# Where a feed-forward's squares lie, and when its result sums are taken, in a fused attention kernel

## The chip, the core and the metric

The kernel runs on one core of one Trainium2 chip. The metric is the device time of one execution in microseconds (us); the kernel before takes 1431.97 us (median of three runs, 1430.68 to 1434.18). A core has TensorE (PE: matmuls into PSUM), VectorE (DVE), ScalarE (ACT), GpSimd (POOL) and SyncE (SP, which here issues the DMAs). Each engine works through its own instructions in the program's order, and semaphores hold an instruction back until its inputs and its output's buffer are ready.

## The reference

Two blocks follow each other. The first is attention with a threshold: of each row of scores only those within tau of the row's maximum are kept. The second normalizes the features, multiplies by two weight matrices with a relu between, and adds the result to its input.

```python
# q, k, v: (8, 8, 576, 64)                                  (cut)
scores = scale * np.matmul(q, k.transpose(0, 1, 3, 2))
thresh = np.max(scores, axis=-1, keepdims=True) - tau
scores = np.where(scores >= thresh, scores, -1000000000.0)
attn = softmax(scores)                       # written out in the original
x = (attn @ v) as (8, 576, 512)
mu = np.mean(x, axis=-1, keepdims=True)
var = np.mean((x - mu) ** 2, axis=-1, keepdims=True)
xn = (x - mu) / np.sqrt(var + 1e-06) * g_ln
ch = np.maximum(xn @ w_ch1, 0.0) @ w_ch2     # (512, 2048), (2048, 512)
return x + ch
```

## The kernel before

The attention of a batch is cut into nine **slots**, 72 in all. A slot does scores (TensorE), the rows' negated maximum `neg` (VectorE), exponentials `e` (ScalarE), threshold and sum (VectorE), the scaling of `e` (GpSimd), and a transpose: `et` on VectorE, written to DRAM as `scr` and read back as `em` in the next slot, where TensorE multiplies it with `v`. Slots are named by batch and step, (2,7) for instance.

The feed-forward of half a batch (a **group** of 288 tokens, 16 groups) is fed to TensorE in small portions between the slots' own matmuls. Group 2b runs its first part from slot (b,6) on, group 2b+1 from slot (b+1,2) on. Scores have PSUM banks of their own; all the rest share a ring of two banks, the tag `ff`.

The first part makes 16 tiles of `hidden`, takes the squares, and at some tile the variance. The reciprocal root follows on VectorE in three steps:

```python
    def first_part(g):
        ...
            nc.scalar.activation(hidden[:, d], p1, func=AF.Relu)
            ...
            if d == (1 if plain else 5):
                sq = ffn.tile([128, NK, TOK], F32, tag="sq", bufs=1, name="sq")
                nc.scalar.activation(sq, xc, func=AF.Square)
                for c in range(1, NK):
                    nc.gpsimd.tensor_tensor(out=sq[:, 0], in0=sq[:, 0], in1=sq[:, c], op=ALU.add)
            if d >= (8 if plain else 11) and rb is None and (part or d == ND - 1):
                var = ps_ff.tile([128, TOK], F32, tag="ff", name="var")
                product(var, lhsT=avg_sb, rhs=sq[:, 0], start=True, stop=True)
                rb = ffn.tile([128, TOK], F32, tag="rb", bufs=2, name="rb")
                nc.scalar.activation(sq[:, 1], var, func=AF.Identity, bias=eps_sb)
                aside.append(lambda: root(rb, sq[:, 1], sq[:, 2]))
                yield 1, 1
```

The second part multiplies by quarters, in seven products instead of eight. The sums of the seven results go into a tile `y`, which has the same tag `sq`, one buffer. They are put into a list, and `drip` deals them out at the end of the slots' quarters, up to 5 or 6 of those that are old enough. `finish` multiplies by the root and adds x; `store` transposes one quarter of the features into a tile `ot`; the sends of all `ot` are issued on SyncE early in the next slot, behind the load of `em`:

```python
    def store(g, m, o):
        ot = ffn.tile([128, TOK], F32, tag="o", bufs=4, name="ot")
        nc.vector.transpose(ot, o)
        stores.append(lambda: send(g, m, ot))
    ...
    # in each slot                                          (cut)
        run(n, 0)                 # em of the slot before is fetched
        run_all(stores)           # then the sends
        second_part(n, 0)
        ...                       # q and k of a later pair: load_qk
        scr = turn_blocks(s, es)  # et, and its write to scr
        drip(5)
        ...                       # v of a later pair: load_v
        second_part(n, 3)
        run_all(aside)
        drip(6)
```

Of the kernel before, what the change touches and what calls it, by code (L numbers as in the profile page):

```python
# [8 lines left out]
F32 = mybir.dt.float32  # L9
# [3 lines left out]
ALU = mybir.AluOpType  # L13
AF = mybir.ActivationFunctionType
# [4 lines left out]
def kernel(  # L19
# [31 lines left out]
    nc = tc.nc  # L51
# [5 lines left out]
    NK = DM // 128  # L57
    ND = DF // 128
    J = 4
    NB = S // 32  # L60
    TOK = S // 2
# [12 lines left out]
    ffn = ctx.enter_context(tc.tile_pool(name="ffn", bufs=2))  # L74
# [6 lines left out]
    eps_sb = consts.tile([128, 1], F32, name="eps_sb")  # L81
# [8 lines left out]
    hidden = consts.tile([128, ND, TOK], F32, name="hidden")  # L90
# [508 lines left out]

    aside, stores, drops = [], [], []  # L600

    def drip(most):


        urgent = [i for i, d in enumerate(drops) if d[0]]
        old = sum(d[1] < now for d in drops)
        n = max(min(most, old), urgent[-1] + 1 if urgent else 0)
        for _ in range(n):
            drops.pop(0)[-1]()

    def run_all(calls):
        now = calls[:]
        calls.clear()
        for fn in now:
            fn()

    def add_to_x(g, m, p2, rb):
        o = ffn.tile([128, TOK], F32, tag="o", bufs=4, name="o")
        nc.vector.tensor_mul(o, p2, rb)
        nc.gpsimd.tensor_tensor(out=o, in0=o, in1=groups[g][:, m], op=ALU.add)  # L620
        aside.append(lambda: store(g, m, o))

    def store(g, m, o):
        ot = ffn.tile([128, TOK], F32, tag="o", bufs=4, name="ot")
        nc.vector.transpose(ot, o)  # L625
        stores.append(lambda: send(g, m, ot))

    def send(g, m, ot):
# [57 lines left out]
    def first_part(g):  # L686


        xc = centred.pop(g)
        rb = sq = None  # L690
        plain = g == 0
        sums_of = differences() if g == 1 else iter(())
        for d in range(ND):
            while conversion.ended < 4 * (d // 4 + 1):
                yield 0, 0
            p1 = ps_ff.tile([128, TOK], F32, tag="ff", name="p1")
            for c in range(NK):
                product(
                    p1, lhsT=w1_sb[c][:, d * 128 : (d + 1) * 128], rhs=xc[:, c],
                    start=(c == 0), stop=(c == NK - 1),  # L700
                )
                if c < NK - 1:
                    yield 1, 1
            nc.scalar.activation(hidden[:, d], p1, func=AF.Relu)  # L704
            next(sums_of, None)
            yield 2, 1
            if d == (1 if plain else 5):
                sq = ffn.tile([128, NK, TOK], F32, tag="sq", bufs=1, name="sq")
                nc.scalar.activation(sq, xc, func=AF.Square)
                for c in range(1, NK):  # L710
                    nc.gpsimd.tensor_tensor(out=sq[:, 0], in0=sq[:, 0], in1=sq[:, c], op=ALU.add)
            if d >= (8 if plain else 11) and rb is None and (part or d == ND - 1):

                var = ps_ff.tile([128, TOK], F32, tag="ff", name="var")
                product(var, lhsT=avg_sb, rhs=sq[:, 0], start=True, stop=True)
                rb = ffn.tile([128, TOK], F32, tag="rb", bufs=2, name="rb")
                nc.scalar.activation(sq[:, 1], var, func=AF.Identity, bias=eps_sb)
                aside.append(lambda: root(rb, sq[:, 1], sq[:, 2]))
                yield 1, 1
        for _ in sums_of:  # L720
            pass
        return rb
# [16 lines left out]
    def second_quarters(g, rb):  # L739

        s2, s3, s4 = more
        b11, b12 = hidden[:, :HD, early], hidden[:, :HD, late]
        b21, b22 = hidden[:, HD:, early], hidden[:, HD:, late]
        y = ffn.tile([128, NK, TOK], F32, tag="sq", bufs=1, name="y")
        part_of = lambda t, i, j: t[:, HM * i : HM * i + HM, (early, late)[j]]
        y11, y12, y21, y22 = (part_of(y, i, j) for i in range(2) for j in range(2))
        done = set()  # L750

        def later(*calls, urgent=None):
            for what, fn, *args in calls:

                def go(what=what, fn=fn, args=args):
                    fn(*args)
                    done.add(what)

                drops.append((urgent, now, go))

        def need(*what):
            while not done.issuperset(what):
                drops.pop(0)[-1]()

        def by_fours(eng, out, in0, in1, op):
            for d in range(0, HD, 4):
                at = (slice(None), slice(d, d + 4))
                eng.tensor_tensor(out=out[at], in0=in0[at], in1=in1[at], op=op)  # L768

        def segment(weights, rhs, out=None):  # L770
            bank = ps_ff.tile([128, HM, HT], F32, tag="ff", name="seg")
            for d in range(HD):
                for m in range(HM):
                    at, end = (d, m), (HD - 1, HM - 1)
                    product(
                        bank[:, m], lhsT=weights[:, m, d], rhs=rhs[:, d],
                        start=at == (0, 0), stop=at == end,
                    )
                    if at != end:
                        yield 2, 0.5  # L780
            if out is None:
                out = ffn.tile([128, HM, HT], F32, tag="part", bufs=4, name="part")
            nc.scalar.copy(out, bank)  # L783
            return out

        def add(eng, out, a, b):
            eng.tensor_tensor(out=out, in0=a, in1=b, op=ALU.add)  # L787

        def finish(eng, i, j=None):

            cols = slice(None) if j is None else (early, late)[j]
            at = (slice(None), slice(HM * i, HM * i + HM), cols)
            z, x = y[at], groups[g][at]
            r = rb[:, cols].unsqueeze(1).to_broadcast(list(z.shape))
            eng.tensor_tensor(out=z, in0=z, in1=r, op=ALU.mult)  # L795
            add(eng, z, z, x)

        dve, pool = nc.vector, nc.gpsimd
        later(("t3", by_fours, pool, b12, b22, b12, ALU.subtract), urgent=pool)
        banks_taken[0] = True  # L800
        yield from segment(w2[0, 0], b11, y11)
        need("t3")
        later(("t2", by_fours, dve, b11, b11, b12, ALU.add), urgent=dve)
        yield 2, 0.5
        p2 = yield from segment(w2[0, 1], b21)
        need("t2")
        later(("t4", by_fours, pool, b21, b21, b11, ALU.subtract), urgent=pool)
        yield 2, 0.5
        p7 = yield from segment(s3, b12)
        yield 2, 0.5  # L810
        yield from segment(s2, b11, y21)
        need("t4")
        later(("t1", by_fours, dve, b11, b22, b11, ALU.subtract), urgent=dve)
        later(
            ("u2", add, pool, y21, y21, y11), ("11", add, pool, y11, y11, p2),
            ("done11", finish, pool, 0, 0),
        )
        yield 2, 0.5
        p4 = yield from segment(w2[1, 1], b21)
        yield 2, 0.5  # L820
        need("t1", "u2", "11")
        p5 = yield from segment(w2[1, 0], b11)
        later(
            ("u4", add, dve, y12, y21, p5), ("u3", add, dve, y21, y21, p7),
            ("22", add, dve, y22, y21, p5), ("21", add, dve, y21, y21, p4),
            ("hi", finish, pool, 1),
        )
        yield 2, 0.5
        last = segment(s4, b22)
        for _ in range(6):  # L830
            yield next(last)
        banks_taken[0] = False
        while waiting_mean:
            mean_of(waiting_mean.pop(0))
        p3 = yield from last
        later(("12", add, dve, y12, y12, p3), ("done12", finish, dve, 0, 1))
        later(*((f"o{m}", store, g, m, y[:, m]) for m in range(NK)))
        yield 2, 0.5

    def ffn_steps(g):  # L840
# [78 lines left out]
    for n in range(NS):  # L919
# [30 lines left out]
        blocks_go = by_blocks(b * HP)  # L950
        diags = weights(es, thr, blocks_go)
        run_all(aside)
        drip(0)
        if n < SLOTS:
            run_all(stores)
        tick(3)
# [21 lines left out]
        if s in (HP, 2 * HP):  # L978
            group_ready(2 * b + (s > HP))
        run_all(aside)  # L980
        drip(5)
        conversion.fetch(2)
        tick(5)
        run(n, 3)
# [4 lines left out]
        second_part(n, 3)  # L989
        tick(6)  # L990
        run_all(aside)
        drip(6)
    while later_calls or queue or aside or stores or drops:
        n += 1
        for i in range(QUARTERS):
            run(n, i)
            second_part(n, i)
            run_all(aside)
            drip(99)
            run_all(stores)  # L1000


# [28 lines left out]
```

## Time and profile before

| | before |
|---|---|
| median time, us | 1431.97 |
| profiled execution, span, us | 1430.3 |
| TensorE busy | 1346.8 us, 94% |
| VectorE, GpSimd, ScalarE busy | 972.4, 591.5, 461.2 us |
| mean granted TensorE clock | 0.986 |
| TensorE's matmuls: first part (p), quarters (seg, three groups) | 528.8 us; 245.8, 123.1 and 63.9 us |
| a slot's neg, in two halves | 1.35 us each |
| an exponential of one of four blocks | 0.74 us |
| relu of one tile; squares of a group | 0.41; 1.16 us |
| a result sum y<-y,part on VectorE; on GpSimd | 0.46; 1.03 us |
| a multiplication by the root of half the features, on GpSimd | 1.48 us |
| a transpose ot | 0.45 us |

A row of a timeline reads: start, length, engine, line, operation, output and inputs, shapes, how many records, and in brackets how long the engine stood idle before it and what ended that. One product of 288 columns is four records of p, 0.516 us (528.8 us by 1024 products); one of 144 columns is four records of seg, 0.256 us. SPq is SyncE's queue of DMA issues: its times are those of issuing, and the landing comes later.

### The profile page before, as it was taken

Reading aid. Unit: us, or ns where it says so; the run is one execution under the profiler, and the core shown is the slowest. Engines: PE = TensorE matmul, PEld = TensorE weight load, DVE = VectorE, ACT = ScalarE, POOL = GpSimd, SP = SyncE. Lnnn points to the kernel's source line nnn. Section 1 sums busy time; section 2 is a strip of 40 time slices with the busy share of each in tenths; the row PEclk is TensorE's granted clock in tenths of the full one; section 3 lists DMA queues with packets and bytes.
Section 4 is the critical chain, followed back from the end, with each engine's and each line's share of the span. In section 5 each row is a group of like instructions: output and inputs, shape, how many; then the busy total and the mean of one; then the engine's idle time right before and its main releaser. Section 6 shows DMA issues by size and latency. Waiting matters only on the chain.

```text
span 1430.3 us, 35964 instructions
## 1 busy us (share of the span) xinstructions
PE 1346.8 (94%) x15048; PEld 995.7 (70%) x15048; DVE 972.4 (68%) x1668; ACT 461.2 (32%) x923; POOL 591.5 (41%) x779
## 2 busy tenths in 40 slices
PE   4889999999999999999999999999999999999996
PEld 3665666857768586867768586776858577685976
DVE  5997958667766677676765777666766677666231
ACT  3886523222222323232232323223232223223120
POOL 2344435534434353443534444433635344343222
PEclk9999999999999999999999999999999999999998
DMA  9622457557864778557864677647775577545211
GB/s 227 174 70 83 91 135 185 143 128 164 180 155 129 157 171 178 153 131 176 185 157 134 155 158 174 162 133 162 173 169 149 139 168 182 142 134 134 68 18 18
DMA packets 466866, 205.53 MB, mean 144 GB/s; under 512 B 275024, under 2 KB 428368, under 8 KB 466704
## 3 DMA queue, kind: packets, MB, share of 16 engines
q1 hardware_dynamic: 461936, 202.64, 59.4%
q8 instruction: 118, 1.93, 0.6%
q10 hardware_dynamic: 4736, 0.59, 0.4%
q14 instruction: 44, 0.36, 0.1%
q0 software_dynamic: 32, 0.00, 0.0%
HBM read 119.41 MB, written 83.76 MB: 142 GB/s over the span
## 4 chain that ended last, share of the span: by engine, by line
PE 73%; DVE 11%; DMA 6%; ACT 4%; SPq 3%; issue 2%; POOL 1%; DVEq 0%; ACTq 0%; POOLq 0%
PE p L101 30%; PE seg L101 24%; PE sc L542 8%; PE sc L385 8%; DMA em<-scr 3%; DVE e L417 2%; DVE y L787 2%; ACT e L410 2%; DVE neg L399 2%; DMA scr<-et 1%; PE tp L101 1%; DVE xc L593 1%; SPq L504 1%; DMA v_in<-in_v_dram 1%; DVE y L795 1%
## 5 line engine op out<-in xcount | busy, mean ns | idle before, releaser
L101 PE MATMUL p<-xc,w 128*64 128x288 f32 x4096 | 528.8, 413 | 28.8 <-ACT hidden L704 26.5
L101 PEld LDWEIGHTS p<-xc,w 128*64 128x64 f32 x4096 | 297.1, 139 | 241.3 <-ACT hidden L704 40.1
L399 DVE TENSOR_REDUCE neg<-sc 128x2 f32<-128x1152 f32 x144 | 188.5, 1350 | 259.6 <-PE sc L385 259.6
L410 ACT ACTIVATE e<-sc,neg 128x576 f32<-128x576 f32 x288 | 196.5, 743 | 267.6 <-DVE neg L399 267.6
L433 POOL TENSOR_SCALAR e<-e,den 128x576 f32<-128x576 f32 x252 | 197.0, 793 | 164.4 <-DVE den L422 164.4
L101 PE MATMUL seg<-hidden,w 128*64 128x144 f32 x3840 | 245.8, 287 | 0.0
L101 PEld LDWEIGHTS seg<-hidden,w 128*64 128x64 f32 x3840 | 235.1, 137 | 8.8 <-issue 6.3
L417 DVE SCALAR_TENSOR_TENSOR e<-sc,thr,e 128x576 f32<-128x576 f32 x288 | 222.0, 810 | 12.2 <-ACT e L410 11.5
L704 ACT ACTIVATE hidden<-p 128x288 f32<-128x288 f32 x256 | 104.6, 412 | 249.1 <-PE p L101 248.7
L385 PE MATMUL sc<-kT,qT 64*128 64x192 f32 (+3 forms) x1024 | 148.9, 424 | 20.0 <-DVE qT L345 10.4
L498 DVE STREAM_TRANSPOSE et<-e 128x1152 f32<-128x1152 f32 x112 | 153.2, 1374 | 12.7 <-POOL e L433 10.9
L403 POOL TENSOR_SCALAR thr<-neg,low_sb 128x2 f32<-128x2 f32 x144 | 42.2, 293 | 280.7 <-DVE neg L399 272.7
L385 PEld LDWEIGHTS sc<-kT,qT 64*128 64x128 f32 x1024 | 94.1, 190 | 70.1 <-issue 16.9
L542 PE MATMUL sc<-em,v_in 128*64 128x256 f32 (+1 forms) x1408 | 131.1, 329 | 6.0 <-DMA em<-scr 6.0
L101 PE MATMUL seg<-hidden,stage 128*64 128x144 f32 x1920 | 123.1, 286 | 0.1
L101 PEld LDWEIGHTS seg<-hidden,stage 128*64 128x64 f32 x1920 | 117.9, 137 | 3.8 <-issue 2.3
L542 PEld LDWEIGHTS sc<-em,v_in 128*64 128x64 f32 x1408 | 86.8, 137 | 40.1 <-DVE ot L625 2.3
L768 POOL TENSOR_TENSOR hidden<-hidden 128x576 f32<-128x576 f32 x60 | 85.8, 1449 | 24.7 <-ACT hidden L704 15.1
L568 POOL TENSOR_TENSOR sum<-sum,x 128x256 f32<-128x256 f32 (+1 forms) x64 | 33.0, 515 | 110.8 <-ACT x L559 108.3
L783 ACT COPY part<-seg 128x288 f32<-128x288 f32 x75 | 30.0, 400 | 145.7 <-PE seg L101 141.4
L768 DVE TENSOR_TENSOR hidden<-hidden 128x576 f32<-128x576 f32 x60 | 48.0, 835 | 33.5 <-PE seg L101 33.5
L559 ACT COPY x<-sc 128x256 f32<-128x256 f32 x60 | 22.3, 372 | 145.2 <-PE sc L542 131.0
(153 smaller groups left out, 1201.6 us busy)
## 6 DMA issues: line engine op xcount, KB each, us to landing
scr<-et SPq DMA_DIRECT2D x252, 288.0 KB, 4.9
em<-scr SPq DMA_DIRECT2D x63, 1024.0 KB, 5.9
out_dram<-ot SPq DMA_DIRECT2D x256, 36.0 KB, 1.9
q_in<-in_q_dram SPq DMA_DIRECT2D x124, 72.0 KB, 5.1
k_in<-in_k_dram SPq DMA_DIRECT2D x120, 72.0 KB, 3.1
v_in<-in_v_dram SPq DMA_DIRECT2D x64, 128.0 KB, 4.5
rest<-scr SPq DMA_DIRECT2D x63, 128.0 KB, 6.0
w<-in_moe_w_ch_dram SPq DMA_DIRECT2D x10, 512.0 KB, 5.8
```

What stands on the lines that cost most here:

```text
L101: nc.tensor.matmul(out[r], lhsT=lhsT[:, r], rhs=rhs, **flags)
L385: nc.tensor.matmul(sc[h][64 * i : 64 * i + 64 if s == HP else 128, at : at + n], lhsT=ql[r] if s == HP else qT[r, half, j * 128 : (j + 1) ...
L399: nc.vector.tensor_reduce(out=neg[:, i], in_=pairs[h], axis=AXL.X, op=ALU.max, negate=True,)
L403: nc.gpsimd.tensor_scalar(out=thr[:, i], in0=neg[:, i], scalar1=-1.0, scalar2=low_sb, op0=ALU.mult, op1=ALU.add,)
L410: nc.scalar.activation(es[:, i], blocks[i], func=AF.Exp, bias=neg[:, i : i + 1])
L417: nc.vector.scalar_tensor_tensor(out=es[:, i], in0=blocks[i], scalar=thr[:, i : i + 1], in1=es[:, i], op0=ALU.is_ge, op1=ALU.mult, accum_o ...
L433: nc.gpsimd.tensor_scalar(out=es[:, i], in0=es[:, i], scalar1=den[:, i : i + 1], scalar2=1.0, op0=ALU.mult, op1=ALU.mult,)
L498: nc.vector.transpose(et[:, :, 64 * h : 64 * h + 64].rearrange("p n (j c) -> p j n c", j=2), es[:, 2 * h : 2 * h + 2].rearrange("p j (n c) ...
L542: nc.tensor.matmul(dst[64 * h : 64 * h + 64], lhsT=vt[:, c, h, :] if c < J else vr[:, h, :], rhs=pick(em[:, c] if c < J else er, hp, h), s ...
L568: nc.gpsimd.tensor_tensor(out=sums[g][:, cols], in0=x[:, 0, cols] if c == 1 else sums[g][:, cols], in1=x[:, c, cols], op=ALU.add,)
L704: nc.scalar.activation(hidden[:, d], p1, func=AF.Relu)
L768: eng.tensor_tensor(out=out[at], in0=in0[at], in1=in1[at], op=op)
```

## The change

The squares are no longer kept in a tile of their own: they go into the last four tiles of `hidden`, which the first part fills only later. They are taken after tile 1, and the variance is asked for from tile 7 on. What ScalarE makes of the variance, and the root's second scratch tile, are new tiles `std` of the tag `o`. So `y` has its buffer to itself for longer, and the sums can be dealt out over two slots. Each entry of the list now has an engine and a cost, and a slot's end has room for 4 units on VectorE and 6 on GpSimd, then 2 and 0. The last multiplication (`done12`) moves from VectorE to GpSimd. The order of the transposes becomes 2, 3, 0, 1. The mean of the next group is let in after 12 steps of the last segment instead of 6.

```diff
-    def drip(most):
+    def drip(room=None, everything=False):
         urgent = [i for i, d in enumerate(drops) if d[0]]
-        old = sum(d[1] < now for d in drops)
-        n = max(min(most, old), urgent[-1] + 1 if urgent else 0)
-        for _ in range(n):
-            drops.pop(0)[-1]()
+        n = urgent[-1] + 1 if urgent else 0
+        room = dict(room or {})
+        while drops:
+            _, when, eng, cost, go = drops[0]
+            if n <= 0 and not everything:
+                if when == now or room.get(eng, 0) < cost:
+                    break
+                room[eng] -= cost
+            drops.pop(0)
+            n -= 1
+            go()
 ...
-            if d == (1 if plain else 5):
-                sq = ffn.tile([128, NK, TOK], F32, tag="sq", bufs=1, name="sq")
+            if d == 1:
+                sq = hidden[:, ND - NK :]
                 nc.scalar.activation(sq, xc, func=AF.Square)
 ...
-            if d >= (8 if plain else 11) and rb is None and (part or d == ND - 1):
+            if d >= 7 and rb is None and (part or d == ND - NK - 1):
 ...
-                nc.scalar.activation(sq[:, 1], var, func=AF.Identity, bias=eps_sb)
-                aside.append(lambda: root(rb, sq[:, 1], sq[:, 2]))
+                two = [ffn.tile([128, TOK], F32, tag="o", bufs=4, name="std") for _ in range(2)]
+                nc.scalar.activation(two[0], var, func=AF.Identity, bias=eps_sb)
+                aside.append(lambda: root(rb, *two))
 ...
+        drip(everything=True)          # before y is allocated
         y = ffn.tile([128, NK, TOK], F32, tag="sq", bufs=1, name="y")
 ...                                    (costs are added to all entries: 1 to 3)
-        for _ in range(6):
+        for _ in range(12):
             yield next(last)
         banks_taken[0] = False         # the next group's mean may take a bank
 ...
-        later(("12", add, dve, y12, y12, p3), ("done12", finish, dve, 0, 1))
-        later(*((f"o{m}", store, g, m, y[:, m]) for m in range(NK)))
+        later(("12", 1, add, dve, y12, y12, p3), ("done12", 2, finish, pool, 0, 1))
+        later(*((f"o{m}", 1, store, dve, g, m, y[:, m]) for m in (2, 3, 0, 1)))
 ...
-        drip(5)
+        drip({nc.vector: 4, nc.gpsimd: 6})
 ...
-        drip(6)
+        drip({nc.vector: 2, nc.gpsimd: 0})
```

More of the change, by code (lines that the diff above doesn't have):

```diff
@@ L620, in add_to_x, with store @@
         nc.gpsimd.tensor_tensor(out=o, in0=o, in1=groups[g][:, m], op=ALU.add)
-        aside.append(lambda: store(g, m, o))
-    def store(g, m, o):
+        aside.append(lambda: store(nc.vector, g, m, o))
+    def store(eng, g, m, o):
         ot = ffn.tile([128, TOK], F32, tag="o", bufs=4, name="ot")
-        nc.vector.transpose(ot, o)
+        eng.transpose(ot, o)
         stores.append(lambda: send(g, m, ot))
@@ L752, in later, with go @@
         def later(*calls, urgent=None):
-            for what, fn, *args in calls:
-                def go(what=what, fn=fn, args=args):
-                    fn(*args)
+            for what, cost, fn, eng, *args in calls:
+                def go(what=what, fn=fn, eng=eng, args=args):
+                    fn(eng, *args)
                     done.add(what)
-                drops.append((urgent, now, go))
+                drops.append((urgent, now, eng, cost, go))
         def need(*what):
@@ L798, in second_quarters @@
         dve, pool = nc.vector, nc.gpsimd
-        later(("t3", by_fours, pool, b12, b22, b12, ALU.subtract), urgent=pool)
+        later(("t3", 3, by_fours, pool, b12, b22, b12, ALU.subtract), urgent=pool)
         banks_taken[0] = True
@@ L802, in second_quarters @@
         need("t3")
-        later(("t2", by_fours, dve, b11, b11, b12, ALU.add), urgent=dve)
+        later(("t2", 3, by_fours, dve, b11, b11, b12, ALU.add), urgent=dve)
         yield 2, 0.5
@@ L806, in second_quarters @@
         need("t2")
-        later(("t4", by_fours, pool, b21, b21, b11, ALU.subtract), urgent=pool)
+        later(("t4", 3, by_fours, pool, b21, b21, b11, ALU.subtract), urgent=pool)
         yield 2, 0.5
@@ L812, in second_quarters @@
         need("t4")
-        later(("t1", by_fours, dve, b11, b22, b11, ALU.subtract), urgent=dve)
+        later(("t1", 3, by_fours, dve, b11, b22, b11, ALU.subtract), urgent=dve)
         later(
-            ("u2", add, pool, y21, y21, y11), ("11", add, pool, y11, y11, p2),
-            ("done11", finish, pool, 0, 0),
+            ("u2", 1, add, pool, y21, y21, y11), ("11", 1, add, pool, y11, y11, p2),
+            ("done11", 2, finish, pool, 0, 0),
         )
@@ L823, in second_quarters @@
         later(
-            ("u4", add, dve, y12, y21, p5), ("u3", add, dve, y21, y21, p7),
-            ("22", add, dve, y22, y21, p5), ("21", add, dve, y21, y21, p4),
-            ("hi", finish, pool, 1),
+            ("u4", 1, add, dve, y12, y21, p5), ("u3", 1, add, dve, y21, y21, p7),
+            ("22", 1, add, dve, y22, y21, p5), ("21", 1, add, dve, y21, y21, p4),
+            ("hi", 3, finish, pool, 1),
         )
@@ L952 @@
         run_all(aside)
-        drip(0)
+        drip()
         if n < SLOTS:
@@ L998 @@
             run_all(aside)
-            drip(99)
+            drip(everything=True)
             run_all(stores)
```

## The prediction

> **What bounds the kernel now.** I read the page's busy table first, then the waits of TensorE, then one group's slots in the timeline. A slot is one scores-and-softmax step; there are 72, written here as batch and step (2,7). All times below are of slots (2,6) to (2,8), one of seven alike places: the first group of features of batches 1 to 7.
>
> ```profile
> PE 1346.8 (94%) x15048; PEld 995.7 (70%) x15048; DVE 972.4 (68%) x1668; ACT 461.2 (32%) x923; POOL 591.5 (41%) x779
> ```
>
> TensorE is busy for 94% of the span and the next engine for 68%, so the time is TensorE's work plus what TensorE waits. The change adds and removes no matmul, so only the waits can move. In total they are:
>
> ```profile
> engine line waited for: us in total, times, longest us
> PE p L101 <- ACT hidden L704: 26.5, 9, 3.3
> PE sc L385 <- DVE e L417: 10.6, 8, 7.2
> PE sc L385 <- DVE qT L345: 10.4, 1, 10.4
> PE sc L542 <- DMA em<-scr: 6.0, 6, 1.8
> ...
> PE mean L101 <- ACT part L783: 2.2, 6, 0.7
> ```
>
> The 10.4 and nearly all of the 10.6 lie in the start. What recurs is the first row: seven waits of 3.25 us, one in each slot (b,7) of batches 1 to 7. The timeline tells why:
>
> ```profile
> 459.41 2.26 DVE L787 TENSOR_TENSOR y<-y,part 128x288 f32<-128x288 f32 x5
> ...
> 461.71 1.54 DVE L795 TENSOR_TENSOR y<-y,rb 128x288 f32<-128x288 f32 x1
> ...
> 463.29 1.55 DVE L787 TENSOR_TENSOR y<-y,x 128x288 f32<-128x288 f32 x1
> 464.87 1.56 DVE L625 STREAM_TRANSPOSE ot<-y 128x288 f32<-128x288 f32 x4
> 466.35 2.58 DVE L399 TENSOR_REDUCE neg<-sc 128x2 f32<-128x1152 f32 x2
> ...
> 469.03 0.71 ACT L704 ACTIVATE hidden<-p 128x288 f32<-128x288 f32 x2
> ...
> 469.49 9.55 PE L101 MATMUL p<-xc,w 128*64 128x288 f32 x64 [3.25 <-ACT hidden L704]
> ```
>
> The scores stood ready at 462.2, but VectorE came to their maximum (neg) at 466.35, after 6.9 us of result sums. ScalarE's exponentials waited for neg, the relu behind them waited too, and with two PSUM banks in the ring TensorE ran dry. The same 64 records take 7.98 us in batches 3, 4 and 6, and 9.55 here, 9.61 in batch 5, 10.75 in batch 7 and about 9.4 in batch 1: behind those waits TensorE's clock record shows 0.50.
>
> **What the Trainium skill says.** *TensorE: Matmul & The Clock Gate*, Part 1 on the clock gate: after an idle window of about 3.4 us TensorE falls to half speed until a busy window has passed. The trace agrees: 3.41 us (once 6.83) at 0.50 behind four of the seven waits. The same page, Architectural detail: ScalarE's queue is strictly first in, first out, so a relu cannot pass an instruction that waits. The trace agrees (469.03 above). *DMA: Bandwidth & Descriptors*, Queues, rings and completion order: on each DMA engine a ring's descriptors are taken in order. The trace agrees: sends issued behind a large load land late, as shown below.
>
> **Part 1: thinner sums, multiplications on GpSimd.** In slot (2,6) only the five additions stay before neg; the multiplication, the addition of x and four transposes (1.54 + 1.55 + 1.56 = 4.65 us) leave that place. But two other things move there. The mean's matmul now comes 6 products later in the last segment: 6 x 0.256 = 1.54 us, less the wait for a bank (0.66 here, 0.3 elsewhere). And in the built program's order the scores of (2,7) come one feature tile earlier, 4 x 0.516 = 2.06 us. Worked through with the durations above: scores end at 459.7, VectorE ends its additions at 462.3, neg's first half is there at 463.6, two exponentials end at 465.1, relu at 465.5. TensorE has two tiles to do from 459.7, until 463.8. So a wait of some 1.8 us stays, and 1.4 goes. With 0.3 us of the mean's wait, and 1.1 us a batch on average of half clock (the excess of those four over 7.98, spread over seven), **part 1 gains 2.8 us in each of seven batches.** ScalarE's squares (1.16 us) now stand between relus and exponentials, and GpSimd's three additions of them (2.4 us) before its scaling of e; both delay VectorE's transposes in that slot, not TensorE.
>
> **Part 2: squares in hidden's last tiles.** y no longer shares a buffer with the squares, which is what allows sums in the next slot. Yet the two small tiles of the variance (std) now come from the pool tag o, which has four buffers, all four taken by the transposed results (ot) of the group before. In the built program's waits I find, in slots (b,7) of all seven batches, that the ScalarE instruction which writes std out of the variance's bank **waits for the four sends of the first ot to land**. These sends stand on the SyncE queue behind the scratch write, the v loads and the em load of the next slot. The queue before:
>
> ```profile
> 479.02 3.89 SPq L504 DMA_DIRECT2D scr<-et  x4
> 482.96 1.61 SPq L130 DMA_DIRECT2D v_in<-in_v_dram  x1
> ...
> 487.79 0.38 SPq L513 DMA_DIRECT2D em<-scr  x1
> ```
>
> From the scratch write's start to the em load 8.8 us pass. In slot (2,7) an em load at 467.25 is followed by sends from 468.23, and the first four take 4.9 to 6.0 us each to land, the last at 474.9: 7.7 us after em was issued. In the changed kernel I put et's end in (2,7) at 473.6, so em goes out at 482.4 and std may be written at 490.1. Its input, the variance, is there at about 478.5. TensorE has one tile (2.06) and the scores of (2,8) (2.15) to do from then and stops at 482.7, because the next tile needs the variance's bank. std takes 0.50 us. **A wait of 490.6 - 482.7 = 7.9 us.**
>
> It does not end there. On VectorE the root's first steps stand before neg of (2,8). They need std, and the second one the sends of the second ot, some 1.7 us later; they end near 493.5. So neg, ready to begin at 482.7, begins 10.8 us late; the exponentials end at 496.3, and the relu behind them at 496.7. Two tiles after resuming TensorE would wait another 2.0 us. Since it resumes cold, at half clock for 3.4 to 6.8 us (2.4 us lost on average), this second wait is mostly hidden; I count 2.9 us for both. **Part 2 costs 10.8 us a batch.**
>
> **Part 3: the second group of a batch.** Its slots had no TensorE wait. Now two products of its last segment fall behind the scores of (b,2), and the second tile needs the bank that ScalarE empties only after two exponentials: neg 1.35, e 1.4, copy 0.4 from the scores' end give 3.4 us, against 0.51 + 2.06 of work: about 0.9 us, six times.
>
> **The end.** Two of four transposes no longer wait for the last sum. The 16 sends take 7.8 us of issue and decide the end; they start about 1 us earlier.
>
> Sum: 7 x (10.8 - 2.8) + 6 x 0.9 - 1 = 60 us, so 1432 + 60 = 1492; I lower it to **1490**, since one or two waits for em (6.0 us in all) may vanish inside the longer slots.
>
> **Rivals.** *A: the wait on the sends is short or hidden.* If they landed by 482, part 2 would cost nothing and the change would gain some 15 us: 1417. For it: sends in the quiet end of the kernel land in 1.7 us. Against it: they stand behind em on the same queue, em cannot be issued before the scratch has landed, and 7.7 us after em was seen. *B: the SyncE queue becomes the bound.* Slot (b,8) gets 16 sends (10.7 us of issue) on top of eight q and k loads and the scratch write, while it had under 3 us of idle issue. With no wait on std, em of (b+1,0) would be some 6 us late and TensorE would wait 4 us for it, seven times: about 1445. I think the wait on std stretches the slot enough to hide this. *C: the neg delay and cold clock add up rather than hide each other*, 2 us more a batch: 1505.
>
> **Range and chances.** The first wait I know to perhaps 2 us (et's end, landing), the clock to 1.5 us, each times seven, and they go together: 1460 to 1512. A alone gives under 1432, and a faster run by over 2% would need more than all recurring waits together: 0.02. Same: 0.06. Slower: 0.92.
>
> **What would show it.** The waits should have a new row near 7 x 8 us, TensorE's tile p on ScalarE's std; ScalarE's std should wait for DMA of ot. The old row of seven 3.25 us should shrink to about 1.8 each. Slot (b,8) should grow from 18.8 to some 28 us and clock records at 0.50 should follow in all seven. Rival B would show as TensorE waiting for em in slot (b+1,0). I am wrong if the sends land before TensorE runs out of tiles, or if the whole of part 1's wait goes.

## The result, and the profile after

| | before | after |
|---|---|---|
| median time, us | 1433.1 (1430.7 to 1435.9) | 1492.9 (1489.8 to 1496.7) |
| ratio after to before | | 1.0418 [1.0383, 1.0453] |
| profiled span, us | 1430.3 | 1489.0 |
| TensorE busy, us | 1346.8 | 1354.3 |
| TensorE idle, span less busy, us | 83.5 | 134.7 |
| mean granted clock | 0.986 | 0.977 |

The change makes the kernel 4.2% slower. The span grew by 58.7 us: TensorE is idle 51.2 us more, and busy 7.5 us more with the same matmuls. The busy row of the changed kernel's page has VectorE 37.8 us lighter, which bought nothing:

```profile
PE 1354.3 (91%) x15048; PEld 995.5 (67%) x15048; DVE 934.6 (63%) x1638; ACT 456.9 (31%) x923; POOL 612.5 (41%) x809
```

The waits of TensorE after the change (waiter, what it waited for, us in total, times, longest):

```profile
engine line waited for: us in total, times, longest us
PE p L101 <- ACT std L725: 57.7, 8, 8.9
...
PE p L101 <- ACT part L792: 8.7, 14, 0.7
PE p L101 <- ACT hidden L711: 6.1, 10, 2.8
PE sc L542 <- DVE e L417: 5.6, 7, 0.9
PE var L101 <- ACT hidden L711: 5.5, 6, 0.9
```

The row that led before (26.5 us on relu) is down to 6.1. One row stands in its place: 57.7 us on std, of which 57.1 are seven waits of 7.4 to 8.9 us, one in each slot (b,8). Three small rows are new. The waits of the other engines say what std itself waited for:

```profile
ACT std L725 <- DMA out_dram<-ot: 83.7, 7, 12.7
...
DVE std L654 <- DMA out_dram<-ot: 18.1, 6, 3.8
```

And the timeline of slots (2,7) and (2,8) shows one such place (start, length, engine, line, operation, in brackets the idle time before it and what ended that):

```profile
469.94 2.62 DVE L399 TENSOR_REDUCE neg<-sc 128x2 f32<-128x1152 f32 x2
...
473.11 8.95 PE L101 MATMUL p<-xc,w 128*64 128x288 f32 x72 [0.26 <-ACT hidden L711]
...
485.02 0.66 PE L101 MATMUL var<-hidden,avg_sb 128*64 128x288 f32 x4
...
489.44 0.45 SPq L513 DMA_DIRECT2D em<-scr  x1
...
490.49 9.91 SPq L639 DMA_DIRECT2D out_dram<-ot  x16
...
497.01 0.50 ACT L725 ACTIVATE std<-var,eps_sb 128x288 f32<-128x288 f32 x1 [11.37 <-DMA out_dram<-ot]
...
497.57 12.71 PE L101 MATMUL p<-xc,w 128*64 128x288 f32 x88 [7.56 <-ACT std L725]
```

Read it from the bottom. TensorE stood 7.56 us for the variance's bank; ScalarE had stood 11.37 us before it could empty that bank into std; the variance had been computed at 485.7. What was missing was the buffer: em, the load issued just ahead of the sends, landed at 495.6, and the first four of the sixteen sends at 496.3 to 496.9, the last of the four 7.5 us after em was issued. The top two lines show what the change was for: in (2,7) relu keeps TensorE waiting only 0.26 us, against 3.25 before. The 88 records after the wait take 12.71 us; at the pace of the undisturbed ones (7.98 us for 64) they would take 10.97. The window of that stretch shows why (length, TensorE busy, granted clock, DMA share, GB/s):

```profile
core 0: us, PE busy (x), PEclk, DMA share, GB/s
...
494.50:501.30 6.80, 3.73 (x16) 0.50 0.60 98
```

Half clock began in the idle time and lasted 6.8 us in all seven places. The 88 records behind the wait take 12.2 to 12.7 us in the seven, 12.45 on average: 1.2 to 1.7 us are lost, 1.5 on average.

### The profile page after: what moved, and what is told of

Its sections match the earlier page's. It is cut to its first block, busy times and chain, and to the rows that moved or that the text cites. A ratio compares the mean times of both kernels' runs of the same rounds, so it can differ in the third digit from the quotient of the medians.

```text
span 1489.0 us, 36024 instructions
## 1 busy us (share of the span) xinstructions
PE 1354.3 (91%) x15048; PEld 995.5 (67%) x15048; DVE 934.6 (63%) x1638; ACT 456.9 (31%) x923; POOL 612.5 (41%) x809
## 4 chain that ended last, share of the span: by engine, by line
PE 67%; DVE 10%; DMA 7%; ACT 5%; POOL 5%; SPq 3%; issue 3%; POOLq 0%; ACTq 0%; DVEq 0%
PE seg L101 25%; PE p L101 24%; PE sc L385 8%; PE sc L542 7%; DMA out_dram<-ot 2%; DVE neg L399 2%; DVE e L417 2%; ACT e L410 2%; DMA scr<-et 2%; POOL e L433 2%; DVE xc L593 1%; DVE et L498 1%; POOL hidden L718 1%; DMA em<-scr 1%; PE tp L101 1%
## 5 line engine op out<-in xcount | busy, mean ns | idle before, releaser
L101 PE MATMUL p<-xc,w 128*64 128x288 f32 x4096 | 533.1, 415 | 73.7 <-ACT std L725 57.7
L385 PE MATMUL sc<-kT,qT 64*128 64x384 f32 (+3 forms) x1024 | 150.1, 424 | 22.2 <-DVE e L417 10.5
L650 DVE TENSOR_SCALAR rb<-std 128x288 int32<-128x288 int32 x16 | 4.9, 305 | 123.9 <-ACT std L725 123.9
```

The source lines that it names most:

```text
L101: nc.tensor.matmul(out[r], lhsT=lhsT[:, r], rhs=rhs, **flags)
L385: nc.tensor.matmul(sc[h][64 * i : 64 * i + 64 if s == HP else 128, at : at + n], lhsT=ql[r] if s == HP else qT[r, half, j * 128 : (j + 1) ...
```

## The experiments

Each ratio is to runs of the kernel before that were taken beside the experiment; their median was 1431.9 us for e1 to e4, 1437.5 for e5 to e8 and 1434.0 for e9 and e10. Compare experiments by their ratios.

**e1: std in buffers of its own.** The changed kernel with one edit, which takes the two std tiles out of the ring that the output tiles use:

```diff
-two = [ffn.tile([128, TOK], F32, tag="o", bufs=4, name="std") for _ in range(2)]
+two = [ffn.tile([128, TOK], F32, tag="part", bufs=4, name="std") for _ in range(2)]
```

> The changed kernel with the two std tiles taken from the tag of the segments' results (part, same size, empty at that time) instead of o; nothing else differs. Theory (the loss is the wait of std on the sends of the transposed results): the seven waits of 7.4 to 8.9 us and the 3.4 us of half clock behind each go, 7 x 11 = 77 us less than the changed kernel: about 1416 us, and slot (b,8) falls from 28 to 17-19 us. Rival B (the SyncE queue, with 16 sends and eight loads in slot (b,8), takes over): TensorE then waits some 4 us for em in slot (b+1,0), about 1445 us. Rival C (the sums over two slots cost by themselves): hardly better than 1493.

Measured: 1436.2 us, ratio to before 1.0026 [1.0008, 1.0043]. All seven std waits are gone and slot (b,8), 27.5 to 28.3 us after the change, takes 18.0. So the buffer ring cost 56.7 us of the 59.8. But the kernel does not become faster than before; the largest waits of e1 past its start are these:

```profile
PE sc L542 <- DMA em<-scr: 10.9, 6, 3.2
PE p L101 <- ACT part L792: 8.7, 14, 0.7
```

The first row holds rival B: with the std wait gone, em comes 0.3 to 3.2 us late in four of the slots (b+1,0), 7.5 us in all. The other 3.4 us lie in batch 1, where the kernel before waits 2.7 us for em too. The theory of 1416 had left this out, rival B of 1445 had it too large. The theory also took 3.4 us of half clock behind each std wait for 3.4 us lost; the loss was 1.5. These two terms, 8.5 us of em (10.9 against 2.4 in the changed kernel) and 7 x 1.9 us of clock, come to about the 20 us by which it missed.

**e3: the ring alone.** The kernel before, with only std and the root's scratch put into the output tiles' tag:

```diff
-nc.scalar.activation(sq[:, 1], var, func=AF.Identity, bias=eps_sb)
-aside.append(lambda: root(rb, sq[:, 1], sq[:, 2]))
+two = [ffn.tile([128, TOK], F32, tag="o", bufs=4, name="std") for _ in range(2)]
+nc.scalar.activation(two[0], var, func=AF.Identity, bias=eps_sb)
+aside.append(lambda: root(rb, *two))
```

> The kernel before with one thing of the change: std and the root's scratch are tiles of the tag o; squares, variance and sums stay where they were. Theory (the tag hurts only because the variance now comes ahead of the sends of the tiles whose buffers it takes): the sends have landed by 480 of the trace and the variance comes at 491, so no wait on sends on ScalarE and the time of the kernel before, 1433 us within 0.5%. Rival (sharing the tag o is the cost as such): seven waits of several us, over 1460 us.

Measured: 1431.3 us, ratio 0.9996 [0.9976, 1.0016]. std waits 1.1 us in all on sends, against 83.7 in the changed kernel, and the only wait of TensorE on std is one in batch 0:

```profile
PE p L101 <- ACT std L718: 0.6, 1, 0.6
```

Sharing the ring costs nothing where the sends have landed before std needs the buffer. It is the ring together with when std is written.

**e4: the variance later.** The changed kernel, std still in the ring, with the squares after tile 5 and the variance from tile 11 instead of 1 and 7:

```diff
-if d == 1:
+if d == (1 if plain else 5):
...
-if d >= 7 and rb is None and (part or d == ND - NK - 1):
+if d >= (7 if plain else 11) and rb is None and (part or d == ND - NK - 1):
```

> The changed kernel with squares and variance at their former places (after tile 5, from tile 11 on), std still of the tag o. Theory: the variance then comes some 8 us later, in slot (b,8), when the first sends have landed or are about to (0 to 1 us of wait): 1415 to 1425 us. If the size of the wait is not set by the distance from variance to landing, it stays near 1490. Rival B as in the first run: TensorE waits about 4 us for em in slot (b+1,0), 1445 us.

Measured: 1438.8 us, ratio 1.0042 [1.0027, 1.0058]. The same ring with a later write of std leaves none of the seven waits (0.9 us in all, mainly in batch 0), and std itself waits 4.9 us on sends instead of 83.7:

```profile
PE p L101 <- ACT hidden L711: 15.1, 8, 2.8
...
PE p L101 <- ACT std L725: 0.9, 2, 0.6
```

Mechanism as expected, time 14 us above the range. As in e1, TensorE waits for em (9.5 us); new is a wait of about 1.9 us on relu in six slots (b,3).

**e2: the mean after six matmuls again**, on top of e1:

```diff
-for _ in range(12):
+for _ in range(6):
```

> As the run before it, and the next group's mean let in after 6 steps of the last segment again instead of 12. Theory: the new short waits of the changed kernel (a tile on the copy of the last segment 0.58 and 0.68 us, the product with v on the masking of e 0.87 us, the variance on a relu 0.91 us) come from the mean's later place, about 1.5 us in each of seven first groups and 1.6 us in each of six second groups: 15 to 20 us less than the run before it, about 1400 us, with the mean's own wait for a bank (0.3 us) back. Rival: they come from the sums dealt out differently, and nothing changes.

Measured: 1426.0 us, ratio 0.9962 [0.9947, 0.9977]. The small new waits on part, on e and of the variance go away, together 20 us in e1. The time fell by 10 us, not by the 15 to 20 expected, because two others grow: 13.6 us for em, 9.3 of them in the six slots (b+1,0), and 2.3 us on relu in each of six slots (b,3). The timeline of e2 in (3,3) shows the second:

```profile
555.55 0.84 DVE L632 STREAM_TRANSPOSE ot<-y 128x288 f32<-128x288 f32 x2 [2.78 <-POOL y L796]
...
557.19 0.48 DVE L632 STREAM_TRANSPOSE ot<-y 128x288 f32<-128x288 f32 x1 [0.80 <-POOL y L796]
557.59 2.58 DVE L399 TENSOR_REDUCE neg<-sc 128x2 f32<-128x1152 f32 x2
...
560.73 7.50 PE L101 MATMUL p<-xc,w 128*64 128x288 f32 x60 [2.31 <-ACT hidden L711]
```

VectorE's output transposes stand in order ahead of neg and wait 2.78 + 0.80 us for GpSimd's last multiplications. This is the price of putting those on GpSimd while dealing the transposes into the same slot.

**e5: the last multiplication back on VectorE**, on top of e2:

```diff
-("done12", 2, finish, pool, 0, 1)
+("done12", 2, finish, dve, 0, 1)
```

> This is the changed kernel with std in buffers of its own and the mean after six matmuls (1426.0 us), and in addition the last multiplication and addition of a group (done12) back on VectorE, as before the change. The theory is that the 2.3-us wait of the first-layer products on relu in slot (b,3), new in those kernels, comes from VectorE: its output transposes stand in order ahead of its row maxima and wait 2.8 us for GpSimd's last multiplications. Two of the four transposes wait for the lower half's finish, which stays on GpSimd, and only the other two for done12, which took 1.6 us there. So theory: the wait shrinks by at most about 0.9 us in six slots, 1421 us (1417 to 1425). Rival: VectorE itself gets 0.9 us more work per group, in the same slots, so nothing is gained: 1426.

Measured: 1419.0 us, ratio 0.9869 [0.9832, 0.9905]. Slot (b,3) falls from 21.0 to 19.4 us: 1.6 us, where 0.9 was expected. The wait for em rises to 17.2 us and takes part of it back.

**e7: thinner still**, on top of e2, so that the transposes come in a slot after the multiplications that they wait for:

```diff
-drip({nc.vector: 4, nc.gpsimd: 6})
+drip({nc.vector: 3, nc.gpsimd: 6})
...
-drip({nc.vector: 2, nc.gpsimd: 0})
+drip({nc.vector: 1, nc.gpsimd: 0})
```

> The repaired kernel of 1426.0 us with the dealing thinner still: room for 3 units of VectorE in the middle of a slot and 1 at its end, instead of 4 and 2. The four output transposes then fall a slot later than the multiplications of the lower half on GpSimd, so VectorE no longer waits for those ahead of its row maxima. Theory: the wait of 2.3 us on relu in (b,3) shrinks to under 0.5, six times, 11 us; but the sends of the first group also come a slot later, in (b+1,0), where queries and keys are loaded, and the wait on the turned blocks there may stay or grow by up to 2 us: 1418 us (1412 to 1428). Rival (the SyncE queue sets the slots around (b+1,0)): 1426 or more.

Measured: **1410.2 us, ratio 0.9813 [0.9771, 0.9854]**, the fastest version of this study: with std in its own buffers, the early mean and this dealing it is 1.9% faster than the kernel before. Its main waits:

```profile
PE sc L385 <- DVE e L417: 11.1, 9, 7.2
PE p L101 <- ACT hidden L711: 10.4, 16, 2.8
...
PE sc L542 <- DMA em<-scr: 5.1, 6, 1.3
```

The first lies nearly all in batch 0; of the second, 3.8 us lie there, and the rest is short waits of 0.3 and 0.7 us. The wait in (b,3) falls from 2.3 to 0.7 us. Most of that for em is gone too, which was not expected: the sends of a group now go out as twelve in (b,8) and four in (b+1,0), and slot (b+1,0) is back to 17.7 to 18.5 us from 18.7 to 22.1 in e2.

**e10: e7 with the last multiplication on VectorE**, the edit of e5:

> The kernel of 1410.2 us with the last multiplication and addition of a group back on VectorE, 0.9 us of its time for 1.6 us of GpSimd's. With the thinner dealing VectorE waits no longer for GpSimd ahead of its row maxima, so theory: nothing left to gain, 1410 us (1405 to 1415). Rival: GpSimd's share of the dealing still delays a slot (a wait on the transposed weights of up to 1.0 us is left in two slots), 1405.

Measured: 1422.0 us, ratio 0.9918 [0.9887, 0.9949]; neither expectation. The operation takes two of VectorE's three units, so two output transposes slip by a slot, and the sends go out as four in (b,8) and twelve in (b+1,0), the reverse of e7. The queue of e7 in (3,0), with the transposes et that its scratch write waits for, and below it that of e10:

```profile
500.57 0.45 SPq L513 DMA_DIRECT2D em<-scr  x1
...
501.62 2.69 SPq L639 DMA_DIRECT2D out_dram<-ot  x4
...
507.70 2.75 DVE L498 STREAM_TRANSPOSE et<-e 128x1152 f32<-128x1152 f32 x2
...
510.99 3.95 SPq L504 DMA_DIRECT2D scr<-et  x4
...
519.65 0.45 SPq L513 DMA_DIRECT2D em<-scr  x1
```

```profile
500.72 8.16 SPq L639 DMA_DIRECT2D out_dram<-ot  x12
...
507.97 2.75 DVE L498 STREAM_TRANSPOSE et<-e 128x1152 f32<-128x1152 f32 x2
...
513.26 3.92 SPq L504 DMA_DIRECT2D scr<-et  x4
...
521.70 0.45 SPq L513 DMA_DIRECT2D em<-scr  x1
...
529.64 1.95 PE L542 MATMUL sc<-em,v_in 128*64 128x256 f32 x16 [2.67 <-DMA em<-scr]
```

et is ready at 510.5 in e7 and 510.7 in e10, but with 8.16 us of sends instead of 2.69 ahead of the loads its write goes out at 511.0 and 513.3. The next em is then issued 2.05 us later, and TensorE waits 2.67 us for it in (3,1). Such waits sum to 13.5 us in e10, 12.1 of them in five slots (b+1,1), and these slots take 20.3 to 25.9 us. In e2, with all sixteen sends in (b,8), the same wait stood one slot earlier, in (b+1,0). It follows the sends: this is rival B's mechanism. The final multiplication on GpSimd is thus a loss under the changed kernel's dealing (e2 against e5, by way of VectorE's wait) and a gain under the thinner one (e10 against e7, by way of the queue).

**e6: squares moved alone.** The kernel before with its old dealing, mean and multiplications, and only the squares in hidden's last tiles at tile 1, variance from tile 7, std in its own buffers (the squares' edits are those of the change; std's is that of e1).

> The kernel before, with only the squares moved (into the last feature tiles, taken at tile 1, variance from tile 7, std in buffers of its own); the dealing of the sums, the final multiplications and the mean are those of before. This is part 2 of the change alone, without its std wait. The theory says that the 3.25-us wait in (b,7) belongs to the dealing of the sums and stays, so the time stays: 1432 us (1428 to 1437). A rival that sees the gain of the repaired kernels in the earlier variance (the 18.8-us slot (b,8) goes to 18.0) expects 0.8 us in seven slots, 1426 us.

Measured: 1447.6 us, ratio 1.0066 [1.0039, 1.0092]: slower than either expectation. The timeline of e6 in (2,7):

```profile
469.58 1.16 ACT L709 ACTIVATE hidden<-xc 128x1152 f32<-128x1152 f32 x1
...
470.64 0.71 ACT L704 ACTIVATE hidden<-p 128x288 f32<-128x288 f32 x2
...
471.10 9.67 PE L101 MATMUL p<-xc,w 128*64 128x288 f32 x64 [4.31 <-ACT hidden L704]
```

The squares at tile 1 fall between the late exponentials and the relus for which TensorE already waits. The 3.25 us become 4.31, and half clock follows in all seven places instead of four.

**e8: the sends on ScalarE's queue**, on top of e2, four at each of four places in a slot (the code that spreads them is left out here):

```diff
-nc.sync.dma_start(out=out[...], in_=ot[...])
+nc.scalar.dma_start(out=out[...], in_=ot[...])
```

> The repaired kernel of 1426.0 us with the 16 sends of a group issued by ScalarE's queue, four in each quarter of the slot, instead of all 16 by SyncE's at its start. Rival B of the prediction says that the sends hold up the scratch writes and loads behind them on SyncE's queue, and that this makes the new waits on the turned blocks, 13.6 us in eight. If so, these fall to the 6 us of the kernel before: 1418 us (1413 to 1424). If ScalarE's issues (about 0.5 us each, 2 us in a quarter) delay its relus and exponentials, the gain is lost again: 1426 to 1440.

Measured: 1480.6 us, ratio 1.0288 [1.025, 1.0326]: much worse than both. Two rows of its timeline in slot (3,3):

```profile
582.76 3.38 ACTq L647 DMA_DIRECT2D out_dram<-ot  x4
...
586.18 0.41 ACT L719 ACTIVATE hidden<-p 128x288 f32<-128x288 f32 x1 [3.02 <-issue]
```

Four issues took 3.38 us and a relu stood behind them for 3.02 us. The wait for em rose to 30.3 us; that late exponentials made the scratch writes late too is the likely reason, not traced further. It says nothing for or against SyncE's sends as the cause of e2's waits for em, because it made ScalarE late; e7 and e10 do.

Its trace does say something about the sends themselves. 51 of them were issued on ScalarE's queue while an em from SyncE's queue was under way. By the landing times of the profile none landed before that em, and they took 5.3 us in the median, against 1.75 us for the other 205. In the changed kernel, with both on SyncE's queue, it was 5.1 us for 112 sends and 1.7 for the other 144. So a buffer was freed only after the em that was under way, from whichever queue the send came; a place behind em on the same queue, as the prediction put it, was not needed for that.

**e9: e7 with std left in the output tiles' ring**, that is, the changed kernel with the two edits of e7 and the early mean.

> The changed kernel with std left in the output tiles' tag, as in the change, but with the dealing of 3 and 1 units of VectorE (instead of 4 and 2) and the mean after six matmuls: the kernel of 1410.2 us, but for std's buffers. With this dealing only three of the four output tiles of the first group are allocated when std is, so std's own buffer is one whose sends landed long before; only the root's scratch takes a buffer of this group, whose sends landed at 486.2 us in the sibling's trace, 0.7 us after VectorE comes to it. Theory (the wait of 7.6 us is the tag together with the number of output tiles in flight): ScalarE's wait on sends disappears, VectorE waits about 1 us that stays off the path, 1412 us (1407 to 1418). Rival (the tag alone makes the wait): about 57 us more than the sibling, 1467.

Measured: 1544.2 us, ratio 1.0758 [1.072, 1.0797]. Both expectations were far off, and the trace tells what they had overlooked:

```profile
498.97 0.45 SPq L513 DMA_DIRECT2D em<-scr  x1
...
500.02 8.59 SPq L639 DMA_DIRECT2D out_dram<-ot  x12
...
506.28 0.48 DVE L632 STREAM_TRANSPOSE ot<-y 128x288 f32<-128x288 f32 x1 [9.26 <-DMA out_dram<-ot]
...
509.82 5.48 PE L101 MATMUL p<-xc,w 128*64 128x288 f32 x24 [7.09 <-ACT hidden L711]
```

std itself no longer waits, as expected. But std and its scratch now take the last two free buffers, and the third output transpose gets that of the first, whose sends land only after em. VectorE waits 9.26 us for them, in order ahead of neg, and TensorE 7.09 us behind neg. This happens in both groups of a batch, 13 times, 145.2 us of VectorE's wait in all. The same four buffers make the same wait, only for whoever asks for the fifth tile.

## Why the prediction was right

It named 1490 us, and 1492.9 came. Step by step:

- **The bound, and part 2's wait.** Right. Seven waits of TensorE on std, in the slot named, 7.4 to 8.9 us, mean 8.15, against 7.9 worked out. e1, e3, e4 and e9 show the cause: it needs the ring, the four output tiles in it, and the early write of std. That the sends land late because they stand behind em on the same queue was too narrow: in e8 those from another queue landed behind it as well.
- **The second wait and the cold clock, 2.9 us together.** The half clock was there in all seven, but the second wait was hidden entirely: the 88 records in (2,8) run without a gap, there and in the other six. What remained was the clock, 12.71 - 10.97 = 1.7 us in (2,8) and 1.5 on average. This term was 1.4 us too large. The scratch's own wait for the second ot is there in six places (18.1 us), off TensorE's path.
- **Part 1's gain, 2.8 us.** The total was right and its form wrong. I left a wait of 1.8 us in (b,7); 0.26 was measured. But two waits came in (b,6) that I had not counted: 0.58 us on part and 0.87 us of the product with v on VectorE's masking. They hold the scores back by 1.45 us, so VectorE is that much less behind. The three make 1.71 us, which fits the wait I foresaw, met earlier. Taken by itself, the wait on relu nearly vanished, and I had named that as a sign of being wrong. With (3.25 + 0.31) before and the 1.1 us of half clock, the gain is 2.9 us.
- **Part 3, 0.9 us in six slots.** Too small. The wait on part was 0.68 us, another of 0.92 us stood before the variance (the row of 5.5 us), and one of 0.25 us before the scores of (b,2): 1.85 us.
- **The end.** Right: from the last matmul to the end 12.7 us instead of 13.8.
- **The sum** from these: 7 x (8.15 + 1.5 - 2.9) + 6 x 1.85 - 1 = 57.4 us, against 58.7 of span. The row for em fell from 6.0 to 2.4 us, as the last 2 us of the prediction supposed, so that some 5 us of small changes stay unassigned. That 1490 came so near is partly luck: the clock term was 10 us too large over the seven places, part 3 was 6 us too small, the wait itself 2.
- **Rival A** is out. **Rival C** is out: the second wait and the cold clock did not add up. **Rival B** was rightly called hidden by the std wait: only 2.4 us for em in the changed kernel, and 10.9 once e1 takes the std wait away. Its 4 us, seven times, were too many: 0.3 to 3.2 in four places.
- **What I did not foresee for the repaired kernel:** with a later mean and the transposes behind GpSimd's multiplications, the dealing itself is worth no more than its new short waits. e1 is 0.3% slower than the kernel before; only with the early mean (e2, e5, e7, e10) is there a gain.

What stays open: whether the four late sends of e7 are what makes its remaining waits for em (5.1 us, of which 2.4 lie in batch 1), what the thinner dealing would cost without the early mean, and whether std's wait goes when the sends are issued ahead of em; none of these was run.

## What to carry to other kernels

Before a tile is put into an existing ring of buffers, list who holds the buffers at that moment and what frees them; where a DMA frees them, see what is under way ahead of it (here a load of 1 MB that landed 5.9 us after its issue in the median), and know that the wait moves to the next taker when the order changes. Dealing work more thinly pays when each piece also lands in a slot after its producer on the other engine; a piece that waits in an in-order engine ahead of the critical reduction costs more than the work it saves. After removing a large wait, look for the one that it was hiding.

## What the runs showed of the hardware that was not expected

A wait of 3.25 us was followed by half clock in four of seven places before, one of 4.3 us in all seven places of e6, and the 7.4- to 8.9-us waits had 6.8 us of half clock each, part of it inside the idle time: the loss per wait was 1.2 to 1.7 us, on average no more than behind the four 3.25-us waits (1.4 to 1.6 us, once 2.8). All four of these measured less than the idle window of about 3.4 us that the prediction counts on, and three waits of the same length had no half clock; what told them apart stays open. And four DMA issues on ScalarE's queue, 0.32 us each at the least and 0.47 in the median of e8, took 3.38 us in slot (3,3) of e8, while relu stood behind them.
